# A fused attention and two-expert kernel on one core: weights decoded in place, one scale for the first output weights, and the pooled sums of twelve head pairs by accumulating transfers

## The chip, the cores and the metric

The kernel runs on one core of one Trainium2 chip. TensorE (PE) multiplies matrices, VectorE (DVE) and ScalarE (ACT) do the elementwise work, SyncE (SP) issues the loads and stores, and GpSimd (POOL) does next to nothing before the change. The metric is the device time of one launch in microseconds.

## What is computed

```python
def sm_attn(qq, kk, vv): ...          # softmax(qq kk^T / sqrt(64)) vv
q_d, k_d, v_d = (a.reshape(4, 8, 144, 4, 64).mean(axis=3) for a in (q, k, v))
out_up = np.repeat(sm_attn(q_d, k_d, v_d), 4, axis=2)       # coarse attention, 144 positions
mask = np.abs(pos[:, None] - pos[None, :]) < 4              # local attention, 576 positions
out_local = softmax(where(mask, scale * q @ k.T, -1e9)) @ v
x = (out_up + out_local).transpose(0, 2, 1, 3).reshape(2304, 512)
x = softplus(x @ w1_in) @ w1_out                            # 512 -> 2048 -> 512, weights in float64
h = x @ w2_in
out = (h * cos(h)) @ w2_out
```

q, k and v are FP32, batch 4, 8 heads, 576 positions. The result must hold far more than 16-bit precision, so each large product is made of three FP16 products of high and low halves (high by high, high by low, low by high).

## The kernel before

**Attention** works on 16 pairs of heads, `pair(b, c)`: batch b, heads 2c and 2c + 1. SP loads three layouts of a pair: `qk` (q and k by head dimension), `vd` (v as 72 partitions by the four positions of a pool) and `vw` (v in windows of 64). VectorE pools by four (`sum1` and `sum2` write `qd`, `sum3` and `sum4` write `vs`). TensorE makes local scores (`A`, tiles `any`) and coarse scores (`Bm`, from `qd`), ScalarE and VectorE the softmaxes, TensorE transposes (`Cm`, `Dm`) and multiplies by v (`Em`); `E1` adds both parts into a tile `xt` of the experts' input.

**Tokens** come in five tiles, four of 512 and one of 256 (`TILES`). Tile 0 needs the four pairs of batch 0, tile 1 those of batches 0 and 1. The sixteen pairs stand at steps written out by hand (`POS1` to `POS3`) among the units of the experts.

**Weights** come as raw 64-bit floats, in eight blocks of 128 x 1024 for each of w1i, w1o, w2i and w2o. `decode` makes FP32 of a block: ScalarE `rebase`, VectorE `join1` and `join2`, ScalarE `bound` (the sum of absolute values, for a safe scale). `scale` gets the maximum over partitions by a spread on TensorE (`allmax`, a broadcast column times `ident_s`) and a reduction on VectorE, and `split` writes the FP16 halves: `high` on ScalarE or VectorE, `low` on VectorE. Before the change the FP32 block is a buffer `x` of its own, and each block of w1i has its own scale. w1o is scaled in four groups of four f, so tile 0's layer 2 is gathered in four accumulations, joined on VectorE (`y_out`).

**Layers.** `unit_in` is one slice f of 128 hidden columns of layer 1 (or of layer 1 of the second expert): twelve matmuls `h<-xt,w1i_t`, then ScalarE and VectorE up to the halves `gh` and `gl`. `l2` and `l4` are the output layers (`any<-g,w1o_t`, `any<-w2o_t,g`). A tile's input needs its maximum, a scale and a split ahead (`x_in`, `y_in`).

**Order.** Nothing is issued where the code stands. Each operation goes into a plan with its engine, a cost and what it reads and writes; `due` gives it a due time by going back from the end, and `order` writes all engines' queues out in one sequence, ready operations by due time. Each engine runs its queue strictly in that order. Where TensorE would be idle early in the program the plan puts in multiplications of zeros (`h<-zero`), which keep its clock up.

Of the kernel before, what the change touches and what calls it, by code (L numbers as in the profile page):

```python
# [13 lines left out]
F32 = mybir.dt.float32  # L14
# [26 lines left out]
POS1 = (2, 5, 8, 11)  # L41
POS2 = (33, 37, 41, 45)
POS3 = (50, 55, 60, 65)
LAT = {"pe": 0.2, "act": 0.145, "dve": 0.13, "pool": 0.06, "sp": 0.95}
NQK, NVD, NVW, NSM, NXB, NST, NGS = 3, 2, 3, 3, 3, 2, 8
# [10 lines left out]
W2STEP = 1  # L56
# [27 lines left out]
class Plan:  # L84
# [36 lines left out]
    def due(self):  # L121
        nxt = 0.0
        for op in reversed(self.ops):
            e, cost = min(op.cost.items(), key=lambda x: x[1])
            end = min([s.due - LAT[e] for s in op.succ], default=0.0)
            if "pe" in op.cost:
                end = min(end, nxt)
                nxt = end - cost
            op.due = end - cost
# [26 lines left out]
    def order(self):  # L156
# [12 lines left out]
        def cool(cost, weight):  # L169

            if now < 0.6 or now > WARM:
                return False
            a0 = now + cost - WIN
            busy[:] = [b for b in busy if b[1] > now - WIN]
            return cost * weight + sum(max(0.0, b - max(a, a0)) * w for a, b, w in busy) < THR
# [91 lines left out]

def dma(kb):
    return {"sp": kb / 353.0}


def build(tc, qk, vw, vd, mask, w1i, w1o, w2i, w2o, out):
# [3 lines left out]
    with ExitStack() as ctx:  # L276
# [12 lines left out]
        def carr(name, n=1):  # L289
            return const.tile([128, n], F32, name=name)  # L290
# [6 lines left out]
        vmx = const.tile([128, NC_], F32, name="vmx")  # L297
# [17 lines left out]
        XB, STG = ring(dp, "x", NXB, [128, 2, 512]), ring(dp, "stg", NST, [128, 2, 512], I64)  # L315
# [52 lines left out]
        def allmax(am, n, red, reads, writes, name):  # L368
# [20 lines left out]
            P.add(pe(0.3 * n), spread, reads, [h], [h], name + " spread")  # L389
# [24 lines left out]
        class Weight:  # L414
            def __init__(self, name, dram):
                self.name, self.dram = name, dram
                self.w = [None] * NF
                self.bd, self.s = carr(f"bd_{name}", NB), carr(f"s_{name}", NF)

            def place(self, pool_):  # L420
                self.t = pool_.tile([128, NF, 2, 512], F16, name=f"{self.name}_t")

            def hi(self, f, a, n):
                return self.t[:, f, 0, a : a + n]

            def lo(self, f, a, n):
                return self.t[:, f, 1, a : a + n]
# [7 lines left out]
            def decode(self, b, after=()):  # L435

                raw, x = STG_.new(), XB_.new()
# [9 lines left out]
                def rebase():  # L447
# [6 lines left out]
                        out=x.t, in_=half(F32, 1), func=AF.Prelu, scale=float(2.0**-112), alpha=-float(2.0**32)  # L454
                    )

                def join1():
                    ts(bits(x.t), bits(x.t), 3, ALU.logical_shift_left)

                def join2():  # L460
                    nc.vector.scalar_tensor_tensor(  # L461
                        out=bits(x.t), in0=half(I32, 0), scalar=29, in1=bits(x.t),
# [3 lines left out]
                def bound():  # L466
                    nc.scalar.activation(
                        out=self.t[:, 2 * b : 2 * b + 2, 0, :].bitcast(BF16), in_=x.t, func=AF.Abs,
                        accum_out=self.bd[:, b : b + 1],
                    )  # L470

                P.add(act(1024), rebase, [raw], [x], [x], nm + " rebase")
                P.add(dve(1024, True), join1, [], [x], name=nm + " join1")
                P.add(dve(1024), join2, [raw], [x], name=nm + " join2")
                P.add(act(1024, 1), bound, [x], [("bd", self.name, b), *self.keys(b)], name=nm + " bound")
                return x
# [15 lines left out]
            def split(self, b, x):  # L492
                w, s = lambda: self.t[:, 2 * b : 2 * b + 2], self.s[:, 2 * b : 2 * b + 1]
                k = ("s", self.name, b)
                nm = f"{self.name}{b}"
                P.add(
                    {**act(1024, 1), **dve(1024, True, 1)}, lambda e: scaled(e, w()[:, :, 0, :], x.t, s),
                    [x, k], self.keys(b), name=nm + " high",
# [762 lines left out]
```

## Time and profile before

| | |
|---|---|
| three runs | 947.76 us median (947.12 to 948.87) |
| profiled execution | 947.95 us |
| its span, first to last instruction | 946.2 us |
| mean granted clock of TensorE | 0.986 |
| busy: TensorE / VectorE / ScalarE / GpSimd | 899.2 / 690.4 / 470.0 / 1.6 us |
| 133 + 72 multiplications of zeros | 34.4 + 18.7 us of TensorE |
| moved by DMA | 58.89 MB, 62 GB/s over the span |

TensorE's busy time is 95% of the span, but an average over stages with different limits; the zero multiplications count in it, too. What a change is worth is read by stages.

### The profile page before, as it was taken

Reading aid. Unit: us, or ns where it says so; the run is one execution under the profiler, and the core shown is the slowest. Engines: PE = TensorE matmul, PEld = TensorE weight load, DVE = VectorE, ACT = ScalarE, POOL = GpSimd, SP = SyncE. Lnnn points to the kernel's source line nnn. Section 1 sums busy time; section 2 is a strip of 40 time slices with the busy share of each in tenths; the row PEclk is TensorE's granted clock in tenths of the full one; section 3 lists DMA queues with packets and bytes.
Section 4 is the critical chain, followed back from the end, with each engine's and each line's share of the span. In section 5 each row is a group of like instructions: output and inputs, shape, how many; then the busy total and the mean of one; then the engine's idle time right before and its main releaser. Section 6 shows DMA issues by size and latency. Waiting matters only on the chain.

```text
span 946.2 us, 14558 instructions
## 1 busy us (share of the span) xinstructions
PE 899.2 (95%) x5809; PEld 469.7 (50%) x5809; DVE 690.4 (73%) x1474; ACT 470.0 (50%) x823; POOL 1.6 (0%) x11
## 2 busy tenths in 40 slices
PE   7899887799999999999999999999999999999797
PEld 4555443345555554444446864444444444444364
DVE  7999999976668776999964566567557656755465
ACT  3464696525445467879866632234224323422243
POOL 0000000000000000000000000000000000000000
PEclk9999998899999999999999999999999999999899
DMA  9557332400122003442200000010001000100100
GB/s 312 164 168 243 119 128 89 171 26 27 31 64 104 1 1 118 152 175 89 90 1 1 1 2 0 1 42 4 1 1 45 1 1 1 45 1 1 44 1 23
DMA packets 13363, 58.89 MB, mean 62 GB/s; under 512 B 1520, under 2 KB 1648, under 8 KB 9200
## 3 DMA queue, kind: packets, MB, share of 16 engines
q1 hardware_dynamic: 13296, 57.97, 17.7%
q8 instruction: 45, 0.74, 0.3%
q14 instruction: 22, 0.18, 0.1%
HBM read 53.25 MB, written 4.72 MB: 61 GB/s over the span
## 4 chain that ended last, share of the span: by engine, by line
PE 74%; DVE 16%; ACT 6%; DMA 2%; issue 1%; SPq 0%; ACTq 0%; DVEq 0%
PE h L897 34%; PE any L1031 19%; PE any L989 17%; DVE td L350 1%; DVE x L461 1%; PE any L724 1%; DVE sm L342 1%; DVE w1i_t L350 1%; DMA vd<-vd 1%; ACT ta L905 1%; DVE xt L350 1%; DMA qk<-qk 1%; DVE rs L602 1%; PE any L675 1%; DVE g L342 1%
## 5 line engine op out<-in xcount | busy, mean ns | idle before, releaser
L897 PE MATMUL h<-xt,w2i_t 128*128 128x512 f16 (+1 forms) x960 | 201.5, 362 | 9.5 <-DVE xt L866 5.3
L897 PE MATMUL h<-xt,w1i_t 128*128 128x512 f16 (+1 forms) x960 | 199.4, 360 | 9.3 <-DVE red L385 6.6
L1031 PE MATMUL any<-w2o_t,g 128*128 128x512 f16 x864 | 197.1, 379 | 0.3 <-DVE g L362 0.3
L989 PE MATMUL any<-g,w1o_t 128*128 128x512 f16 (+1 forms) x864 | 179.5, 357 | 2.3 <-ACT ed L646 1.4
L897 PEld LDWEIGHTS <-w2i_t 128*128 128x128 f16 x960 | 95.3, 99 | 105.7 <-issue 11.5
L897 PEld LDWEIGHTS <-w1i_t 128*128 128x128 f16 x960 | 93.8, 98 | 102.6 <-issue 14.2
L989 PEld LDWEIGHTS <-w1o_t 128*128 128x128 f16 x960 | 93.7, 98 | 89.1 <-issue 4.8
L930 ACT ACTIVATE ta<-h,quarter,i 128x512 f32<-128x512 f32 (+1 forms) x80 | 58.8, 735 | 155.2 <-PE h L897 155.2
L1031 PEld LDWEIGHTS <-g 128*128 128x128 f16 x864 | 84.5, 98 | 100.6 <-DVE g L362 0.8
L342 DVE TENSOR_TENSOR g<-td,g 128x512 f16<-128x512 f32 (+1 forms) x152 | 96.3, 634 | 8.0 <-ACT g L360 1.3
L905 ACT ACTIVATE ta<-h,i 128x512 f32<-128x512 f32 (+1 forms) x80 | 51.4, 642 | 80.7 <-PE h L897 67.4
L935 DVE TENSOR_SCALAR tb<-ta 128x512 f32<-128x512 f32 (+1 forms) x80 | 32.0, 400 | 77.6 <-ACT ta L930 77.1
L945 DVE SCALAR_TENSOR_TENSOR td<-h,r,tc 128x512 f32<-128x512 f32 (+1 forms) x80 | 55.8, 697 | 42.9 <-ACT tc L941 41.2
L941 ACT ACTIVATE tc<-ta 128x512 f32<-128x512 f32 (+1 forms) x80 | 46.9, 586 | 74.5 <-DVE ta L342 74.5
L350 DVE SCALAR_TENSOR_TENSOR td<-ta,sg,tb 128x512 f32<-128x512 f32 (+1 forms) x64 | 43.7, 682 | 48.4 <-ACT ta L917 48.0
L917 ACT ACTIVATE ta<-ta,one 128x512 f32<-128x512 f32 (+1 forms) x80 | 54.2, 680 | 2.0
L362 DVE CAST g<-td 128x512 f16<-128x512 f32 (+1 forms) x124 | 49.4, 398 | 8.0 <-PE any L989 0.8
L342 DVE TENSOR_TENSOR ta<-ta,tb 128x512 f32<-128x512 f32 (+1 forms) x80 | 51.0, 638 | 2.4
L909 ACT ACTIVATE tb<-h,r 128x512 f32<-128x512 f32 (+1 forms) x80 | 51.1, 639 | 0.0
L913 ACT ACTIVATE ta<-ta 128x512 f32<-128x512 f32 (+1 forms) x80 | 46.9, 588 | 0.0
L453 ACT ACTIVATE x<-stg 128x1024 f32<-128x1024 f32 x32 | 36.8, 1149 | 14.1 <-DVE w2i_t L350 3.8
L1195 PE MATMUL h<-zero 128*128 128x512 f16 x133 | 34.4, 393 | 5.3 <-POOL zero L1186 2.4
(147 smaller groups left out, 848.8 us busy)
## 6 DMA issues: line engine op xcount, KB each, us to landing
qk<-qk SPq DMA_DIRECT2D x16, 589.0 KB, 6.6
stg<-w1i SPq DMA_DIRECT2D x8, 1024.0 KB, 7.0
stg<-w1o SPq DMA_DIRECT2D x8, 1024.0 KB, 6.4
stg<-w2i SPq DMA_DIRECT2D x8, 1024.0 KB, 4.8
stg<-w2o SPq DMA_DIRECT2D x8, 1024.0 KB, 4.8
vw<-vw SPq DMA_DIRECT2D x16, 320.0 KB, 4.3
vd<-vd SPq DMA_DIRECT2D x16, 288.0 KB
out<-osb SPq DMA_DIRECT2D x18, 256.0 KB, 2.1
```

Source lines behind the costliest of these rows:

```text
L342: eng[e].tensor_tensor(out=out, in0=in0, in1=in1, op=op)
L350: nc.vector.scalar_tensor_tensor(out=out, in0=raw, scalar=s, in1=other, op0=ALU.mult, op1=op)
L362: nc.vector.tensor_copy(out, in_)
L897: nc.tensor.matmul(h.t[:, 0:n], l, r, start=(i == 0), stop=(i == 11))
L905: act(n, 1, True), lambda: nc.scalar.activation(out=a(), in_=h.t[:, 0:n], func=AF.Abs, scale=col(o.i1, f)),
L909: act(n, 1, True), lambda: nc.scalar.activation(out=b(), in_=h.t[:, 0:n], func=AF.Relu, scale=col(o.r1, f)),
L913: act(n), lambda: nc.scalar.activation(out=a(), in_=a(), func=AF.Exp, scale=-1.0),
L917: act(n, 1), lambda: nc.scalar.activation(out=a(), in_=a(), func=AF.Ln, bias=one),
L930: act(n, 2, True), lambda: nc.scalar.activation(out=a(), in_=h.t[:, 0:n], func=AF.Identity, scale=col(o.i2, f), bias=quarter), [h, *sc], [ ...
L945: dve(n, False, 1), lambda: nc.vector.scalar_tensor_tensor(out=td.t[:, 0:n], in0=h.t[:, 0:n], scalar=col(o.r1, f), in1=r(), op0=ALU.mult, ...
L989: nc.tensor.matmul(a.t[:, i, 0:n], l, r, start=(first and j == 0), stop=(last and j == 2))
L1031: nc.tensor.matmul(a.t[:, i], l, r, start=(f == 0 and j == 0), stop=(f == NF - 1 and j == 2))
```

## The change

Five things change together. **(1)** A block is decoded in the memory of its own FP16 halves: the weight tile has room for one half-block more, the FP32 values of block b lie over the low halves of b and the high halves of b + 1, and `split` goes through them in order. `bound` writes its by-product over the raw block. The buffers `x` and their limit go; tile 0's raw input gets a buffer of its own instead of lying in w1i. **(2)** w1i is scaled in two groups of four blocks and w1o, once all eight blocks are decoded, by one scale (`first_scale`), so layer 2 of tile 0 is one accumulation over 16 f. w2i and w2o are scaled two blocks at a time. **(3)** For batches 1 to 3 (`DA`), `qd` and `vs` come straight from memory: for each of the four positions of a pool GpSimd issues three transfers, the first time as copies, then three times adding in FP32 onto what is there. `vd` isn't loaded for them and the four sums on VectorE go. `qs` and `vr` are the same q, k and v laid out for it beforehand. **(4)** The maxima are BF16 instead of FP32, and some work that either engine could do is fixed on ScalarE (`either`). **(5)** `due` counts the load of VectorE and ScalarE, too; the pairs' positions move; the second expert prepares tile t + 1 at unit 8 of tile t, and keeps four output groups back before tile 4.

```diff
-POS1 = (2, 5, 8, 11)
+POS1 = (6, 10, 15, 20)
+W2G = 2
+QKP, VP, DA = (), (), (1, 2, 3)
+YIN = 8
+DR4 = 4
+A_W, A_C, A_X, A_G = True, True, True, False
+CAP = ("pe", "dve", "act")
+OUT0 = 8
+IN0 = ((0, 4), (4, 4))
...
+def either(a, d, first):
+    return a if first else {**a, **d}
...
-        ident_s = const.tile([128, 128], F32, name="ident_s")
+        ident_s = const.tile([128, 128], BF16, name="ident_s")
...
+                self.t = pool_.tile([128, 1024 * (NF + 1)], F16, name=f"{self.name}_t")
...
+            def floats(self, b):
+                return self.t[:, 2048 * b + 1024 : 2048 * b + 3072].bitcast(F32).rearrange("p (m e) -> p m e", m=2)
...
                 P.add(
-                    {**act(1024, 1), **dve(1024, True, 1)}, lambda e: scaled(e, w()[:, :, 0, :], x.t, s),
-                    [x, k], self.keys(b), name=nm + " high",
+                    either(act(1024, 1), dve(1024, True, 1), self.first and A_W), lambda e: scaled(e, self.his(b), self.floats(b), s),
+                    [x, k], self.keys(b) + over, name=nm + " high",
                 )
...
+            elif b in DA:
+                def term(r):
+                    kw = {"accum_op": ALU.add} if r else {}
+                    heads = qd.t.rearrange("p (m i) -> p m i", m=3)
+                    nc.gpsimd.dma_start(out=heads[0:64, 0:3:2, :], in_=qs[b, c, r, 0:64], **kw)
+                    nc.gpsimd.dma_start(out=heads[64:128, 1:3, :], in_=qs[b, c, r, 64:128], **kw)
+                    nc.gpsimd.dma_start(out=vs.t, in_=vr[b, c, r], **kw)
+                for r in range(4):
+                    aop(
+                        {"pool": 3.0}, lambda r=r: term(r), [], [qd, vs, "qd", "vs"], [] if r else [qd, vs], f"{nm}term{r}",
+                    )
...
-            m = 4 if t == 0 else NF
-            first, last = f % m == 0, f % m == m - 1
+            first, last = f == 0, f == NF - 1
...
+        def grp_out():
+            for b in range(NB):
+                W1O.decode(b)
+            W1O.scale(0, 4)
+            first = [("sc0", b) for b in range(NB)]
             W1O.scale(
-                2 * g, 2, group_scale(g), [("sc0", 2 * g), ("sc0", 2 * g + 1)],
-                [("sc0g", g)] + [("s", "w1o", 2 * g), ("s", "w1o", 2 * g + 1)],
+                4, 4, first_scale(), first + [("s", "w1o", b) for b in range(4)],
+                [("sc", 0)] + [("s", "w1o", b) for b in range(NB)],
             )
-            for i in range(2):
-                W1O.split(2 * g + i, xs[i])
+            for b in range(NB):
+                W1O.split(b)
...
-            if f == 0:
-                if t == 4:
-                    drain(0)
+            if i == 0:
                 y_in(t)
+            if f == YIN and t < 4:
+                y_in(t + 1)
+            if t == 4 and f == 0:
+                drain(DR4)
```

GpSimd's queue held no transfer; now it holds 144. The first two terms of the first pair of batch 1, with what each waits for (`DMASW` are the counters of its own earlier transfers; DVE and PE waits are for the last readers of the buffers):

```order
L648 DMA qd_117<-qs 64x2x144 [waits DVE_49,PE_49]
L649 DMA qd_117<-qs 64x288
L650 DMA vs_120<-vr 72x256 [waits PE_49]
L648 DMA qd_117<-qs 64x2x144 [waits DMASW0_49]
L649 DMA qd_117<-qs 64x288 [waits DMASW1_49]
L650 DMA vs_120<-vr 72x256 [waits DMASW2_49]
```

Each transfer that adds waits until the one of the term before into the same bytes has landed; two more terms like the second follow, and then the next pair into `qd_118`.

VectorE before, at the first output weights, from the reduction of the first group's maxima to its first low half:

```order
L339 TENSOR_SCALAR s_w1o<-red 128x4
L362 CAST xt_84<-td_96 128x512
L339 TENSOR_SCALAR s_w1o<-s_w1o 128x4
L342 TENSOR_TENSOR xt_84<-td_96,xt_84 128x512
L810 TENSOR_TENSOR gs<-lc_159,s_w1o 128x4
L350 SCALAR_TENSOR_TENSOR td_96<-ta_93,lc_159,tb_95 128x512
L811 TENSOR_REDUCE kg<-gs 128x1
L350 SCALAR_TENSOR_TENSOR xt_83<-xt_83,sx_179,xs_97 128x512
L339 TENSOR_SCALAR ikg<-kg 128x1
...
L356 TENSOR_SCALAR w1o_t<-x_106,s_w1o 128x2x512
L356 TENSOR_SCALAR xs_97<-xt_83,sx_179 128x512
L350 SCALAR_TENSOR_TENSOR w1o_t<-x_106,s_w1o,w1o_t 128x2x512
```

And after the change, from the second half of the common scale to the first low half:

```order
L380 TENSOR_SCALAR s_w1o<-red 128x8
L844 TENSOR_TENSOR xt_84<-any_89,up_129 128x128
L380 TENSOR_SCALAR s_w1o<-s_w1o 128x8
L383 TENSOR_TENSOR xt_85<-td_96,xt_85 128x512
L911 TENSOR_TENSOR gs<-lc_160,s_w1o 128x16
L391 SCALAR_TENSOR_TENSOR td_96<-ta_92,lc_160,tb_94 128x512
L912 TENSOR_REDUCE k_166<-gs 128x1
L403 CAST xt_86<-td_96 128x512
L380 TENSOR_SCALAR ik_167<-k_166 128x1
...
L383 TENSOR_TENSOR xt_86<-td_96,xt_86 128x512
L391 SCALAR_TENSOR_TENSOR w1o_t<-w1o_t,s_w1o 128x1024
```

The low half reads and writes `w1o_t` alone, all sixteen f share one scale, the high half ahead of it has gone to ScalarE, and the splits of tile 1 (`xt_83` with `xs_97`) have moved behind it. It was the 375th instruction of VectorE and is the 255th.

TensorE before, where tile 4 of the second expert begins (`w2o_t` with `g`: layer 4 of tile 3; `am`: the maximum of tile 4; `xt_86`: its input):

```order
L1031 LDWEIGHTS g_105
L1031 MATMUL any_88<-w2o_t,g_105 128x512
L378 MATMUL h_91<-ident_s,am_4_245 128x128
L897 LDWEIGHTS w2i_t
L897 MATMUL h_90<-xt_86,w2i_t 128x256
```

And after it:

```order
L1124 LDWEIGHTS g_101
L1124 MATMUL any_88<-w2o_t,g_101 128x512
L998 LDWEIGHTS w2i_t
L998 MATMUL h_91<-xt_86,w2i_t 128x256
...
L998 MATMUL h_90<-xt_86,w2i_t 128x256
L1124 LDWEIGHTS g_102
L1124 MATMUL any_87<-w2o_t,g_102 128x512
```

The spread of tile 4's maximum now stands several hundred rows earlier, and two units of tile 4 lie among the layer-4 groups of tile 3, four of which (`g_102` and on) come behind them.

## Rows read from the trace of the kernel before

**Rows 1.** Busy time by stretches of the span, all engines (count), granted clock, DMA share.
```profile
core 0: us, PE busy (x) PEld busy (x) DVE busy (x) ACT busy (x) POOL busy (x), PEclk, DMA share, GB/s
0.00:167.20 167.20, 143.33 (x1496) 82.74 (x1496) 157.70 (x376) 101.88 (x201) 1.64 (x11) 0.98 0.52 173
167.20:173.70 6.50, 0.79 (x2) 0.53 (x3) 6.50 (x14) 4.49 (x11) 0.00 (x0) 0.68 0.37 115
...
218.40:350.00 131.60, 130.57 (x1103) 71.72 (x1101) 97.37 (x210) 72.20 (x147) 0.00 (x0) 1.00 0.12 41
...
708.00:730.00 22.00, 21.09 (x100) 9.69 (x98) 15.00 (x38) 9.65 (x14) 0.00 (x0) 1.00 0.13 48
...
875.00:904.00 29.00, 22.25 (x104) 11.64 (x103) 12.72 (x40) 7.05 (x13) 0.00 (x0) 0.82 0.10 36
```

**Rows 2.** VectorE's groups to 167.2 us: count, busy us, mean ns, idle before.
```profile
L461 DVE SCALAR_TENSOR_TENSOR x<-stg,x 128x1024 int32<-128x1024 int32 x11 | 13.3, 1211 | 0.0
L350 DVE SCALAR_TENSOR_TENSOR td<-ta,lc,tb 128x512 f32<-128x512 f32 x16 | 11.9, 741 | 0.0
L350 DVE SCALAR_TENSOR_TENSOR w1i_t<-x,s_w1i,w1i_t 128x1024 f16<-128x1024 f32 x8 | 10.2, 1279 | 0.1
L342 DVE TENSOR_TENSOR qt<-qk 128x288 f32<-128x288 f32 x20 | 8.2, 451 | 3.9 <-DMA qk<-qk 3.9
L342 DVE TENSOR_TENSOR sm<-any,nm 128x640 f32<-128x640 f32 x10 | 8.1, 810 | 0.0
...
L339 DVE TENSOR_SCALAR x<-x 128x1024 int32<-128x1024 int32 x11 | 7.5, 685 | 0.0
...
L342 DVE TENSOR_TENSOR vd<-vd 72x512 f32<-72x512 f32 x10 | 6.7, 674 | 0.9 <-DMA vd<-vd 0.9
L342 DVE TENSOR_TENSOR qd<-qt 64x144 f32<-64x144 f32 x20 | 5.9, 297 | 0.1
...
L342 DVE TENSOR_TENSOR vs<-vd 72x256 f32<-72x256 f32 x10 | 3.9, 392 | 0.0
L362 DVE COPY aTd<-any 72x576 f32<-72x576 f32 x5 | 3.7, 747 | 0.3 <-PE any L692 0.3
...
L342 DVE TENSOR_TENSOR qd<-qt 128x144 f32<-128x144 f32 x10 | 3.1, 309 | 0.2
L350 DVE SCALAR_TENSOR_TENSOR xt<-xt,sx,xs 128x512 f16<-128x512 f32 x4 | 3.0, 745 | 0.0
...
L385 DVE TENSOR_REDUCE red<-h 128x1 f32<-128x128 f32 x10 | 2.8, 276 | 0.0
```

**Rows 3.** TensorE's groups, the first two behind 173.7 us alone, the others over the span.
```profile
L897 PE MATMUL h<-xt,w1i_t 128*128 128x256 f16 x192 | 23.1, 273 | 0.0
...
L378 PE MATMUL h<-ident_s,am 128*128 128x128 f32 x16 | 3.3, 287 | 0.2 <-DVE red L385 0.2
...
L576 PE MATMUL any<-qk 64*64 64x64 f32 x640 | 13.0, 223 | 0.0
L630 PE MATMUL any<-qd 128*96 128x144 f32 x72 | 10.9, 288 | 0.4 <-DVE sm L342 0.4
L572 PE MATMUL any<-mask_sb,ident_b 128*128 128x320 bf16 x32 | 7.1, 304 | 0.0
```

**Rows 4.** TensorE in order of time where tile 4 begins: start us, us, what.
```profile
887.89 0.39 PE L378 MATMUL h<-ident_s,am 128*128 128x128 f32 x2
891.53 0.49 PE L897 MATMUL h<-xt,w2i_t 128*128 128x256 f16 x3 [3.25 <-DVE xt L866]
...
900.29 2.72 PE L897 MATMUL h<-xt,w2i_t 128*128 128x256 f16 x12 [1.48 <-DVE td L945]
```

**Rows 5.** Transfers: count, KB each, median us from issue to landing.
```profile
qk<-qk SPq DMA_DIRECT2D x16, 589.0 KB, 6.6
stg<-w1i SPq DMA_DIRECT2D x8, 1024.0 KB, 7.0
out<-osb SPq DMA_DIRECT2D x18, 256.0 KB, 2.1
```

**Rows 6.** The issue of one transfer on SP: ns min/median/max, first and last start.
```profile
L531 SPq DMA_DIRECT2D vd<-vd x16: 321/321/437, 1.6 to 260.4; - x16
```

More of the change, by code (lines that the diff above doesn't have):

```diff
@@ L121, in due @@
     def due(self):
[L122 to L129, printed above, removed]
+        pre = {op: [] for op in self.ops}
+        for op in self.ops:
+            for x in op.succ:
+                pre[x].append(op)
+        left = {op: len(op.succ) for op in self.ops}
+        end = {op: 0.0 for op in self.ops}
+        free = dict.fromkeys(("pe", "dve", "act", "pool", "sp"), 0.0)
+        pes = [op for op in self.ops if "pe" in op.cost]
+        ready = [op for op in self.ops if not left[op] and "pe" not in op.cost]
+        n = len(self.ops)
+        while n:
+            best = None
+            cand = list(ready)
+            if pes and not left[pes[-1]]:
+                cand.append(pes[-1])
+            for op in cand:
+                for e in op.cost:
+                    x = (min(free[e], end[op]) if e in CAP else end[op], op.n)
+                    if best is None or x > best[0]:
+                        best = (x, op, e)
+            (x, _), op, e = best
+            if op is (pes[-1] if pes else None):
+                pes.pop()
+            else:
+                ready.remove(op)
+            op.due = x - op.cost[e]
+            if e in CAP:
+                free[e] = op.due
+            n -= 1
+            for q in pre[op]:
+                end[q] = min(end[q], op.due - LAT[min(q.cost, key=lambda z: q.cost[z])])
+                left[q] -= 1
+                if not left[q] and "pe" not in q.cost:
+                    ready.append(q)
         first = {}
@@ L466, in bound @@
                 def bound():
[L467 to L472, printed above, removed]
+                    out = raw.t.rearrange("p m e -> p (m e)")[:, 0:256].bitcast(BF16)
+                    with nc.allow_low_precision(reason="a bound, for the choice of a scale"):
+                        nc.scalar.activation(
+                            out=out.rearrange("p (m e) -> p m e", m=2), in_=self.floats(b), func=AF.Abs,
+                            accum_out=self.bd[:, b : b + 1],
+                        )
+                P.add(act(1024), rebase, [raw], [x], [], nm + " rebase")
                 P.add(dve(1024, True), join1, [], [x], name=nm + " join1")
                 P.add(dve(1024), join2, [raw], [x], name=nm + " join2")
-                P.add(act(1024, 1), bound, [x], [("bd", self.name, b), *self.keys(b)], name=nm + " bound")
-                return x
+                P.add(act(1024, 1), bound, [x], [("bd", self.name, b), raw], name=nm + " bound")
             def scale(self, b0, n, then=(), reads=(), writes=()):
@@ L507, in build @@
         W1O.place(wp)
-        STG_, XB_ = STG, XB
+        STG_ = STG
+        raw0 = [dp.tile([128, 512], F32, name=f"raw{c}") for c in range(NC_)]
         att_ops = []
@@ L641, in B1a @@
             def B1a():
[L642 removed]
+                nc.scalar.activation(
+                    out=nd.t[0:RB, 0:3], in_=nd.t[0:RB, 0:3], func=AF.Copy, scale=float(2.0**-7)
+                )
             def B2():
@@ L1111, in place2 @@
             dp2 = ex.enter_context(tc.tile_pool(name="dp2", bufs=1))
-            for s, n, shape, dt in ((STG2, NST2, [128, 2, 512], I64), (XB2, NXB2, [128, 2, 512], F32)):
-                s.tiles += [dp2.tile(shape, dt, name=f"{s.name}{i}") for i in range(n)]
+            STG2.tiles += [dp2.tile([128, 2, 512], I64, name=f"stg2{i}") for i in range(NST2)]
         def place3():
```

237 lines of the change are left out of this document (134 added, 103 removed).

## The prediction

> **What bounds the kernel now.** I read the busy time of the engines by stretches first [rows 1]. Three regimes show. Up to about 174 us VectorE is the bound: it is busy 157.7 of the first 167.2 us, while ScalarE is busy 101.9 and TensorE's 143.3 contain the zero matmuls that only keep it warm. Between 167.2 and 173.7 TensorE does almost nothing (0.79 us) and VectorE works without a break: the first layer-2 matmul of tile 0 waits for decoding. From 173.7 us on TensorE is the bound, 130.57 of 131.6 us in the stretch after 218.4, with short holes where a tile of the second expert begins (21.09 of 22.0) and one large one near the end (22.25 of 29.0 us at a granted clock of 0.82). So what the change takes off VectorE counts only ahead of 173.7 us, and behind it only TensorE's own work and holes count. I work out the two parts apart, split at the first layer-2 matmul of tile 0.
>
> **Part one, VectorE's queue up to the first low half of w1o.** That instruction ended at 167.2 us. The 376 VectorE instructions to there fall into 62 groups; the first and largest are in [rows 2]. Their busy columns add up to 183.9 us, because neighbours overlap, so one microsecond of a column is worth 167.2 / 183.9 = 0.909 us of time. The order of the changed kernel has 255 instructions to the same point (375 in that of before). What differs, in busy columns [rows 2]:
> - Pooled sums: 8.2 + 5.9 + 3.1 + 6.7 + 3.9 = 27.8 us for ten pairs; only the four of batch 0 keep them: 27.8 × 0.6 = -16.7.
> - Seven groups go to ScalarE (the copies of aTd, aT and up, the high halves of w1i and w1o, two of xhi0, the small scaling of nd), from 3.7 down to 0.7 us: -11.0.
> - Scaling: 14 small groups, from 2.8 (ten reductions over 128) to 0.1 us, together 11.5. Two scalings of four blocks for each matrix leave four reductions over 512 (a 640-wide one takes 0.81 us, so about 0.65 each) and some 20 steps at 0.16 to 0.19: 6.1. -5.4.
> - Placed behind this point now: three splits of tile 1 (3.0 for four, with their xhi and copies 5.2), the last two units of tile 0 (two sixteenths of 11.9, and their halves: 3.3), one pair's softmax (three at 0.81 and smaller ones: 5.0), one low half (1.3): -14.8.
> - Placed ahead of it now: five more decoded blocks, since all eight of w1o must be decoded before their common scale: 5 × (13.3 + 7.5) / 11 = +9.5.
>
> Sum: -38.4, so 145.5 × 0.909 = 132 us instead of 167.2. ScalarE takes over about 15 us there and would be busy some 117 of 132, where it was 102 of 167; an engine that full hands over late. If nothing of that delays VectorE the point is at 132, if all 11 us that moved come back as waits it is at 143; I take a third, 136, as ScalarE's queue still has 15 us of slack. In TensorE's order a spread and two small groups of a pair stand ahead of the first layer-2 matmul, and they need nothing that comes later, so 137 instead of 173.7 us: **36.7 us gained**. The 6.5 us hole behind 167.2 goes with it: it was a wait for the second group's scale, and there is no second group.
>
> **Part two, TensorE from there.** Before it lasts 946.2 - 173.7 = 772.5 us.
> - The spreads of the maxima read FP32 and now BF16, and there are 24 single matmuls where 56 records stood. 16 of them cost 3.3 us [rows 3], 56 about 11; a BF16 one over 320 columns costs 7.1 / 32 = 0.22, so 128 columns about 0.09, together 2.2: -8.9.
> - Tile 4 of the last expert: its input is prepared while tile 3 still runs, and four layer-4 groups stay behind as work. Before, the maximum's spread ended at 888.3 and the run of layer 4 began again at 903.0; in between stand only 36 matmuls 256 wide, with waits of 3.25 and 1.48 us and some at half speed [rows 4]; at the 23.1 / 192 = 0.12 us of their like [rows 3] they are 4.3 us of work. 14.7 - 4.3 = 10.4 us lost, of which I take 9.5 as saved. The three holes at tiles 1 to 3, 22.0 - 21.09 = 0.9 each [rows 1], go too: -2.7.
> - Fewer pairs have been begun by then: three score blocks ((7.1 + 13.0) / 16 = 1.26 us each), one coarse score (10.9 / 12 = 0.9) [rows 3] and one small transpose group (taken at 0.6) are still to do: +5.3. Four zero matmuls fewer: -1.0.
>
> Sum: 755.7. The six additions on VectorE that gathered tile 0's output over four groups were hidden behind TensorE, so removing them is worth nothing, and so are the pooled sums of the last seven pairs. Decoding in place frees a staging buffer one ScalarE instruction later than before; a load takes about 7 us [rows 5], 16 blocks in 132 us leave 8 for each and there are two buffers, so it costs nothing, and would cost a few us if loads grew slower beside the new transfers.
>
> **The new transfers.** Nothing in this trace shows an accumulating transfer or one issued by GpSimd. Each pair of batches 1 to 3 has four terms; a term's three transfers wait for those of the term before, so four landings follow one another, and the coarse score on TensorE, with all that is queued behind it, waits for the last. Two buffers of qd let GpSimd run two pairs ahead at most. The nearest rows are landings of 2.1 us (256 KB, nothing beside it) and 6.6 us (589 KB beside other loads) [rows 5]; these transfers have 74 KB. So a pair takes 4 × 2.1 = 8.4 us at least, and 26.4 us at the upper end, plus issues of 0.32 to 0.44 us each by SP's row [rows 6]. The time that it has: 151 of the 255 VectorE instructions stand between the coarse scores of the fifth and the ninth pair, so 151 / 255 × 133 / 4 = 20 us for a pair. By size I take a landing of 3 us, so 13 to 16 us for a pair, hidden, and 4 us in all for late hand-overs (one for each of the first four pairs).
>
> The Trainium skill ("DMA: Bandwidth & Descriptors", Anatomy of one DMA, SWDGE path) gives about 2.0 us fixed plus bytes over 436 GB/s for such a transfer; an estimate from that page is 2.2 us for 74 KB and 8.7 us for a pair, so hidden. Against the change speaks "SBUF — State Buffer" (SBUF: two separate sides): while VectorE runs in a two-port mode GpSimd cannot write descriptors, and a transfer of 620 ns took 3100 ns; 2.5 us more on every one of four landings would make an estimated 18.8 us of a pair, and the sum would stay. No run here shows either.
>
> **Sum.** 137 + 755.7 + 4 = 896.7 us of span. The profiled execution took 1.75 us more than its span (947.95 against 946.2) and stood 0.2 above the median, so **898 us**.
>
> **Rivals.**
> - *GpSimd's chain sets the pace* (ends slower). From P us for a pair, stage one loses 5 × (P - 20), as four pairs and the ninth queue behind one another. The later seven pairs come every 131.6 / 7 = 18.8 us [rows 1], and the 40 us of layer 2 on tile 0 give GpSimd a lead, so they lose 6 × (P - 18.8) - 40 when that is positive. At P = 28 (landings of 6.6 and an issue of 0.4): 40 + 15, so about 953. It decides from P = 27.5, a term of 6.9 us. For it: transfers of this size in many short rows, beside weights. Against: the long landings belong to transfers eight times as large.
> - *GpSimd's issues hold up VectorE.* 60 transfers are issued in stage one. If each held a VectorE instruction for as long as SP takes for an issue, 0.32 to 0.44 us [rows 6], VectorE would lose 19 to 26 us: 917 to 924. For it: VectorE is full there, so nothing hides it. Against: GpSimd stood still here but for the first microseconds, so no row shows that the two meet. The page on SBUF has it that the one that starts second blocks wholly, for two-port operations alone.
> - *A wait in the new order that I have not named*, worth half the gain: about 923.
>
> **How the numbers follow.** Forecast 0.70, between 886 (VectorE waits half as much as before, 128.5 + 1, all 10.4 us of tile 4 saved, no late hand-over: 129.5 + 754.8 + 1.6) and 912 (143 + 1, the three holes stay, 8 for hand-overs: 144 + 758.4 + 8 + 1.6). Issues that hold up VectorE 0.16, an unnamed wait 0.04, GpSimd's chain 0.10. From 884 to 932 holds the first three and leaves out the chain and part of the tails. A measurement of this kernel tells about 0.2% from no change (947.12 to 948.87 in three runs): faster 0.88, within it 0.02, slower 0.10.
>
> **What would show it.** Right: the first layer-2 matmul of tile 0 at 133 to 144 us, VectorE over 90% busy ahead of it; TensorE 99% busy from there to the last tile and no hole over 1 us where tile 4 begins; the coarse scores of batch 1 not waiting for a DMA. Wrong: waits of TensorE for the transfers into qd in each pair; VectorE's instructions of known shape longer than their rows of before; ScalarE the releaser of VectorE's idle time for more than 10 us in stage one.

## The result: 907.8 us, and the profile after

The changed kernel took 907.82 us (median of four runs, 902.35 to 912.29) beside 947.81 of the kernel before: a ratio of 0.9575, interval 0.9521 to 0.9628. 898 was predicted, with a range of 884 to 932. The execution that was profiled is the slowest of the four, 912.29 us with a span of 910.3. The runs of this kernel differ by 1.1%, those of before by 0.2%.

Busy time of the changed kernel's engines by stretches (columns as in [rows 1]):

```profile
0.00:157.10 157.10, 127.98 (x1282) 73.66 (x1283) 129.67 (x256) 112.87 (x224) 62.30 (x84) 0.93 0.75 219
157.10:350.00 192.90, 192.90 (x1552) 102.03 (x1550) 125.39 (x255) 103.31 (x203) 58.20 (x72) 1.00 0.29 61
...
395.00:430.00 35.00, 33.34 (x158) 15.18 (x157) 32.52 (x81) 32.99 (x51) 0.00 (x0) 1.00 0.49 178
430.00:845.00 415.00, 415.00 (x2123) 206.89 (x2121) 270.98 (x540) 169.21 (x278) 0.00 (x0) 1.00 0.02 9
845.00:875.00 30.00, 30.00 (x191) 18.47 (x190) 19.34 (x44) 11.78 (x24) 0.00 (x0) 1.00 0.01 2
```

The first layer-2 matmul of tile 0 begins at 157.07 us by the timeline, where 137 was predicted and 173.7 stood before. Behind it TensorE has no hole until 350 us and none from 430 to 875; the holes of before at the tiles of the second expert are gone [rows 1, 4]. That part lasts 910.3 - 157.1 = 753.2 us, where 755.7 was predicted. Ahead of it VectorE, the bound of part one before the change, is now idle for 27.4 of 157.1 us.

TensorE in order of time where tile 4 of the second expert begins (start us, us, what; an idle time ahead would stand in brackets):

```profile
850.99 2.75 PE L1124 MATMUL any<-w2o_t,g 128*128 128x512 f16 x12
853.58 2.78 PE L998 MATMUL h<-xt,w2i_t 128*128 128x256 f16 x24
856.20 2.11 PE L1124 MATMUL any<-w2o_t,g 128*128 128x512 f16 x9
```

What VectorE waited for is in its groups to 157.1 us (count, busy us, mean ns, then idle time ahead of the group and its releaser):

```profile
L391 DVE SCALAR_TENSOR_TENSOR td<-ta,lc,tb 128x512 f32<-128x512 f32 x14 | 10.4, 742 | 3.4 <-ACT ta L1018 3.3
L391 DVE SCALAR_TENSOR_TENSOR w1i_t<-w1i_t,s_w1i 128x1024 f16<-128x1024 f32 x8 | 10.2, 1276 | 0.6 <-ACT w1i_t L395 0.4
...
L380 DVE TENSOR_SCALAR w1o_t<-w1o_t 128x1024 int32<-128x1024 int32 x8 | 5.8, 731 | 8.0 <-ACT w1o_t L508 8.0
L380 DVE TENSOR_SCALAR w1i_t<-w1i_t 128x1024 int32<-128x1024 int32 x8 | 5.5, 688 | 3.5 <-ACT w1i_t L508 3.5
```

The instructions themselves are as long as before (742 and 1276 ns; 741 and 1279 in [rows 2]). The two lines with 8.0 and 3.5 us are `join1`, which waits for ScalarE's `rebase` (L508) of the same block. The waits of the first 160 us (in all, times, longest) say what `rebase` waits for:

```profile
POOL qd L648 <- DMA qd<-qs: 44.7, 19, 6.6
POOL qd L648 <- PE h L731: 22.7, 1, 22.7
POOL qd L648 <- PE any L731: 12.6, 1, 12.6
...
ACT w1i_t L508 <- DMA stg<-w1i: 7.7, 5, 2.7
...
ACT w1o_t L508 <- DMA stg<-w1o: 5.9, 5, 2.5
```

It waits for the raw block's load, by ScalarE's own waits for 13.6 us (7.7 and 5.9). TensorE is nowhere named as waiting for a transfer into `qd`; GpSimd, on the contrary, waits 35.3 us for TensorE to read a buffer of `qd`, so its chain is hidden. By the timeline its first six pairs begin at 25.1 to 129.4 us, one every 20.9 us; the last issue of the second ends at 67.4 and its coarse score begins at 74.4. The transfers (the queues, q1 with the loads and q0 with GpSimd's transfers: packets, MB, share of 16 engines; then as in [rows 5]), first over the whole span:

```profile
q1 hardware_dynamic: 12288, 54.43, 17.0%
q0 software_dynamic: 12864, 10.63, 7.6%
...
stg<-w1i SPq DMA_DIRECT2D x8, 1024.0 KB, 8.3
...
qd<-qs POOLq DMA_DIRECT2D x96, 72.0 KB, 3.0
...
vs<-vr POOLq DMA_DIRECT2D x48, 72.0 KB, 3.7
```

and then from 20 to 150 us:

```profile
q1 hardware_dynamic: 4463, 22.79, 49.7%
q0 software_dynamic: 6432, 5.31, 26.1%
...
stg<-w1o SPq DMA_DIRECT2D x8, 1024.0 KB, 6.8
stg<-w1i SPq DMA_DIRECT2D x6, 1024.0 KB, 6.9
...
qd<-qs POOLq DMA_DIRECT2D x48, 72.0 KB, 4.8
...
vs<-vr POOLq DMA_DIRECT2D x24, 72.0 KB, 5.1
```

A median stands on those loads alone whose landing the profile shows, and these are few: four of the eight w1i blocks here, one in the kernel before. The 8.3 us contain two loads that were issued at 11.4 and 11.9 us and landed after 9.3 and 12.7, before GpSimd's first transfer. From 20 us on a block of w1i lands after 6.9 us and one of w1o after 6.8, where 7.0 and 6.4 stood before, each from one block. So these rows do not show that loads became slower than before the change. What they show is that the loads are now on the chain of work that ended last: its pieces up to 157.1 us are loads of w1i and w1o for 36.4%, some 57 us.

### The profile page after: what moved, and what is told of

It reads as the page before. It is cut to its first block, busy times and chain, and to the rows that moved or that the text cites. A ratio compares the mean times of both kernels' runs of the same rounds, so it can differ in the third digit from the quotient of the medians.

```text
span 910.3 us, 14298 instructions
## 1 busy us (share of the span) xinstructions
PE 874.4 (96%) x5694; PEld 454.7 (50%) x5694; DVE 633.7 (70%) x1273; ACT 478.5 (53%) x856; POOL 120.5 (13%) x155
## 3 DMA queue, kind: packets, MB, share of 16 engines
q1 hardware_dynamic: 12288, 54.43, 17.0%
q0 software_dynamic: 12864, 10.63, 7.6%
## 4 chain that ended last, share of the span: by engine, by line
PE 80%; DMA 9%; ACT 7%; DVE 3%; issue 1%; SPq 0%; ACTq 0%
PE h L998 36%; PE any L1124 20%; PE any L1089 18%; DMA stg<-w1i 4%; DMA stg<-w1o 3%; ACT stg L524 2%; PE any L830 2%; DMA stg<-w2o 1%; PE any L819 1%; DMA stg<-w2i 1%; PE any L731 1%; DMA vw<-vw 1%; PE any L677 1%; PE any L779 1%; ACT ta L1006 1%
## 5 line engine op out<-in xcount | busy, mean ns | idle before, releaser
L998 PE MATMUL h<-xt,w2i_t 128*128 128x512 f16 (+1 forms) x960 | 199.0, 358 | 0.0
L1089 PE MATMUL any<-g,w1o_t 128*128 128x512 f16 (+1 forms) x864 | 176.9, 356 | 0.0
L648 POOL DMA_DIRECT2D qd<-qs x48 | 47.2, 984 | 158.8 <-PE any L731 77.0
L403 DVE CAST g<-td 128x512 f16<-128x512 f32 (+1 forms) x128 | 51.1, 399 | 7.3 <-PE any L1089 0.4
L650 POOL DMA_DIRECT2D vs<-vr x48 | 53.0, 1104 | 14.3 <-DMA vs<-vr 11.3
L649 POOL DMA_DIRECT2D qd<-qs x48 | 50.0, 1041 | 7.7 <-DMA qd<-qs 7.6
```

What stands on the lines that cost most here:

```text
L403: nc.vector.tensor_copy(out, in_)
L649: nc.gpsimd.dma_start(out=heads[64:128, 1:3, :], in_=qs[b, c, r, 64:128], **kw)
L650: nc.gpsimd.dma_start(out=vs.t, in_=vr[b, c, r], **kw)
L998: nc.tensor.matmul(h.t[:, 0:n], l, r, start=(i == 0), stop=(i == 11))
L1089: nc.tensor.matmul(a.t[:, i, 0:n], l, r, start=(first and j == 0), stop=(last and j == 2))
```

## The experiments

The miss is in part one, and three theories stood for it. **Theory 1:** the accumulating transfers take the DMA engines that the weights need. **Theory 2:** ScalarE, which was given more work, hands over late. **Theory 3:** a raw block is freed only by ScalarE's `bound`, which now writes over it, so the two raw buffers set the pace of the loads. All kernels below were timed against the kernel before on the same chip; each ratio has its 95% interval. Only the run with thin transfers and, up to the second expert, the one with the old order keep every engine's order of instructions. Every other edit lets the plan write a new order from the first 20 to 50 us on, so a few us between two of those kernels can come from the order as well as from the edit.

**The changed kernel again, and its transfers made thin.** Queues, issues and waits of the second kernel are those of the changed one; the adding terms move 8 rows each.

```diff
-                    kw = {"accum_op": ALU.add} if r else {}
+                    kw, n, m = ({"accum_op": ALU.add}, 8, 8) if r else ({}, 64, 72)
...
+                    nc.gpsimd.dma_start(out=heads[0:n, 0:3:2, :], in_=qs[b, c, r, 0:n], **kw)
+                    nc.gpsimd.dma_start(out=heads[64 : 64 + n, 1:3, :], in_=qs[b, c, r, 64 : 64 + n], **kw)
+                    nc.gpsimd.dma_start(out=vs.t[0:m], in_=vr[b, c, r, 0:m], **kw)
```

> The changed kernel once more, beside the other three on one chip. In its first profiled execution, 912.3 us, the first layer-2 matmul of tile 0 stood at 157.1 us instead of the predicted 137. Every theory: a median of 902 to 912 us, a spread near 1% again. If the executions differ in part one alone, the stretch behind that matmul keeps its 753 us and the matmul moves with the time of the execution.

> The order, the issues and the waits are those of the changed kernel; the three adding terms of each pair move 8 rows each instead of 64, 64 and 72, so three quarters of most pooled sums of batches 1 to 3 are left out of the output. Theory 1 (the adding transfers share the DMA engines with the weights, whose loads land late): the issue-to-landing time of w1i and w1o comes back from 8.3 and 6.8 us to at most 7.0 and 6.4, the first layer-2 matmul of tile 0 comes 10 us or more earlier than in the changed kernel beside it, the time is 893 to 898 us and its spread under 0.4%. Theory 2 (ScalarE, which was given more work, hands over late) and theory 3 (a raw block is freed only by ScalarE's bound, so its buffer sets the pace of the loads): the time stays within 3 us of the changed kernel, 902 to 912, with its spread.

The changed kernel took 908.64 us (905.11 to 912.53, ratio 0.9585, 0.9558 to 0.9612), the first layer-2 matmul at 156.9 us. With thin transfers it took 899.18 (898.20 to 901.76; 0.9484, 0.9463 to 0.9504), the matmul at 144.2. Its queue and transfers over the span, its loads from 20 to 150 us, and the same two waits of VectorE:

```profile
q0 software_dynamic: 5376, 3.63, 2.2%
...
qd<-qs POOLq DMA_DIRECT2D x24, 72.0 KB, 2.5
qd<-qs POOLq DMA_DIRECT2D x72, 9.0 KB, 2.7
...
stg<-w1o SPq DMA_DIRECT2D x8, 1024.0 KB, 5.1
stg<-w1i SPq DMA_DIRECT2D x6, 1024.0 KB, 5.1
...
DVE w1i_t L380 <- ACT w1i_t L508: 2.5, 1, 2.5
DVE w1o_t L380 <- ACT w1o_t L508: 1.8, 3, 1.3
```

Nothing but the rows moved has changed (GpSimd's issues last 0.90 to 1.01 us in the median, 0.95 to 1.11 before), so what the terms move costs 9.5 us. From 20 us on the loads land 1.8 and 1.7 us earlier than in the changed kernel, their part of the chain that ended last falls from 36.4% of 157.1 us to 11.4% of 144.2, and VectorE's waits for `rebase` shrink from 11.5 to 4.3 us. Theory 1 holds, with 899 a little above the time that it forecast.

Not all of it is waiting. TensorE does the same work from its last wait to the first layer-2 matmul in both kernels, and it took 16.6 us in the changed kernel (140.5 to 157.1) and 12.4 with thin transfers (131.8 to 144.2). The changed kernel first, then the thin one:

```profile
140.51 1.86 PE L1300 MATMUL any<-zero 128*128 128x512 f16 x4 [2.10 <-ACT aTd L401]
...
143.47 2.60 PE L830 MATMUL any<-aT,vw 64*64 64x58 f32 x44
...
146.40 9.46 PE L998 MATMUL h<-xt,w1i_t 128*128 128x512 f16 x36
```

```profile
131.84 1.02 PE L1300 MATMUL any<-zero 128*128 128x512 f16 x4 [1.84 <-ACT aTd L401]
...
133.44 1.49 PE L830 MATMUL any<-aT,vw 64*64 64x58 f32 x44
...
135.09 7.93 PE L998 MATMUL h<-xt,w1i_t 128*128 128x512 f16 x36
```

The granted clock was 0.53 of full speed from 140 to 150 us in the changed kernel, close to the lower of its two levels (1.2 instead of 2.4 GHz), after TensorE had been busy for 1.63 of the 5 us ahead; in the thin one it was 1.00 from 125 to 150. So 4.2 of the 12.9 us between these two executions are a slow clock behind TensorE's idle time; the rest had come about up to its last wait.

**A scratch tile for the by-product of `bound`.**

```diff
+        dump = dp.tile([128, 1024], BF16, name="dump")
...
-                    out = raw.t.rearrange("p m e -> p (m e)")[:, 0:256].bitcast(BF16)
+                    out = dump if self.first else raw.t.rearrange("p m e -> p (m e)")[:, 0:256].bitcast(BF16)
...
-                P.add(act(1024, 1), bound, [x], [("bd", self.name, b), raw], name=nm + " bound")
+                P.add(act(1024, 1), bound, [x], [("bd", self.name, b)] + ([] if self.first else [raw]), name=nm + " bound")
```

> The by-product of bound for w1i and w1o goes into a scratch tile of its own, so that a raw block is free again after VectorE's second joining step, as before the change. Theory 3 (the raw buffer, freed late, sets the pace): SP's waits for ScalarE ahead of weight loads (34.5 us for 10 of them) shrink to a third, ScalarE's waits for a raw block (7.7 and 5.9 us) go, the first layer-2 matmul of tile 0 comes 8 us or more earlier, 893 to 899 us. Theories 1 and 2: the loads are issued earlier but land no earlier by more than 3 us at the end of part one, 900 to 910 us.

It took 912.91 us (912.04 to 916.20; 0.9634, 0.9612 to 0.9656), 4 us more than the changed kernel beside it. SP's waits ahead of the weight loads, to 157 us, no longer name `bound` (first line, of the changed kernel), but VectorE's `join2`:

```profile
SPq L495 <- ACT stg L524: 34.5, 10, 9.2
...
SPq L496 <- DVE w1i_t L517: 31.0, 8, 6.8
SPq L496 <- DVE w1o_t L517: 21.1, 6, 5.3
```

They are longer than the 34.5 us for ScalarE that they replace, and ScalarE waits for w1i 9.1 us where it was 7.7. The first layer-2 matmul is 21 us earlier, at 135.5, but the plan has put less ahead of it: TensorE is busy 107.25 us there, 36.48 of them with zeros, so 70.8 us of work are done, 91.0 (127.98 - 37.03) in the changed kernel. The part behind it lasts 774.6 us instead of 753.2. So that `bound` holds the buffer is not the cause. That there are only two raw buffers is not cleared by this run: SP still waits for one to come free 14 times ahead of the 16 loads, and no run had a third. It also says that the place of that matmul alone is no measure, unless the order ahead of it is the same.

**Work that may go to VectorE again.**

```diff
-A_W, A_C, A_X, A_G = True, True, True, False
+A_W, A_C, A_X, A_G = False, False, False, False
```

> The work that the change fixed on ScalarE (the high halves of w1i and w1o, copies of the transposes, splits of tile inputs) may go to VectorE again, as the plan finds it; VectorE gets 18 instructions more. Theory 2 (ScalarE hands over late): waits of VectorE for ScalarE's high halves (8.0 and 3.5 us) go, the first layer-2 matmul of tile 0 comes 5 us or more earlier, 895 to 902 us. Theories 1 and 3: VectorE was full without them, so the matmul comes later by some of the 18 instructions' 8 to 12 us and the time is 905 to 918 us.

910.95 us (910.05 to 911.94; 0.9604, 0.9586 to 0.9622). VectorE's waits for `rebase` are 4.5 and 3.1 us, shorter, and the matmul stands at 154.9, and still nothing is gained. So theory 2 isn't borne out as it was put. The run doesn't show that ScalarE's load costs nothing, as VectorE, busy for 132 of the first 150 us there, got the work back; the last run below, with more of it on ScalarE, was slower.

**Part (3) taken out,** all pairs pooled on VectorE as before the change; then batch 1 alone taken out.

```diff
-QKP, VP, DA = (), (), (1, 2, 3)
+QKP, VP, DA = (), (), ()
```

> All sixteen pairs are pooled on VectorE again and vd is loaded for them; everything else is as in the changed kernel. It prices part (3) of the change. If the transfers' data cost 9.5 us, as the run with 8 rows said, then taking the transfers out gives these back and adds the pooled sums of six pairs to VectorE's queue, 16.7 us of columns or 15 of time: 910 to 918 us. If the 9.5 us came from something else than shared DMA engines, the whole 15 us show: 918 to 926. If VectorE is no longer the bound of part one, neither shows: 897 to 903.

> The kernel without accumulating transfers once more, beside the two others on one chip: 901 to 906 us, a ratio to the kernel before of 0.950 to 0.955.

> Batch 1 is pooled on VectorE, batches 2 and 3 by transfers, so that the first 100 us have few transfers beside the weights. Four pairs of VectorE's sums come back (11.1 us of columns, 10 of time) against some two thirds of 9.5 us of shared DMA engines: 909 to 914 us by the theory of shared engines; 917 to 920 if VectorE alone counts; under 903 if the transfers cost more early, beside the first weights, than the sums do.

Without the transfers: 903.56 us (901.60 to 905.15; 0.9524, 0.9504 to 0.9545), and timed again 902.91 (902.37 to 904.61; 0.9518, 0.9498 to 0.9538). With batch 1 alone taken out (`DA = (2, 3)`): 903.78 (901.19 to 911.33; 0.9538, 0.9504 to 0.9573). The first and the last are below what every theory expected that assigned VectorE's sums their full time, and the repetition agrees with the first: part (3) as a whole costs about 5 us. A stretch and two transfers of the first run without it:

```profile
100.00:150.00 50.00, 45.15 (x462) 24.88 (x459) 49.40 (x91) 46.78 (x80) 0.00 (x0) 1.00 0.36 128
...
stg<-w1i SPq DMA_DIRECT2D x8, 1024.0 KB, 5.3
stg<-w1o SPq DMA_DIRECT2D x8, 1024.0 KB, 5.0
```

and the same stretch of the changed kernel:

```profile
100.00:150.00 50.00, 38.44 (x256) 20.39 (x255) 39.67 (x74) 40.48 (x75) 23.59 (x29) 0.86 0.66 178
```

From 100 to 150 us, where w1o is decoded, VectorE does 49.4 us of work instead of 39.7, although it has the sums of six more pairs to make: it no longer waits for loads, and the granted clock of TensorE is 1.00 there instead of 0.86. That VectorE is full again agrees with its being the bound of part one once nothing else delays it.

**Batch 1 pooled on TensorE** (`QKP, VP, DA = (1,), (1,), (2, 3)`, branches that the kernel already had).

> Batch 1 is pooled on TensorE (eight FP32 multiplications by the identity for q and k of a pair, and the coarse product over the four unpooled v), batches 2 and 3 by transfers. TensorE has some 30 us of multiplications of zeros and 30 us of idle time ahead of the first layer-2 matmul, ScalarE gets four placements of about 0.85 us. Theory of shared engines: 900 to 905 us, with the loads of w1i at 7.0 to 7.5 us. Rival (theory 2, ScalarE): 908 to 914. Second rival: the FP32 multiplications stand in TensorE's order ahead of work that waits for TensorE, so 905 to 912 with more of TensorE's time and fewer zeros.

911.01 us (910.70 to 912.43; 0.9610, 0.9591 to 0.9629), which lies in the range of the second rival, but also in that of the first, so the time alone doesn't tell them apart. TensorE to 144.2 us:

```profile
L629 PE MATMUL any<-qk,ident 128*128 128x144 f32 x64 | 17.2, 436 | 0.0
```

TensorE's zeros fell from 37.0 us to 25.9, but the sums of q and k alone take 17.2 us there. GpSimd issues nothing before 99.6 us in this run, and from 20 us on the loads of w1i still land after 7.5 us: a late landing has other causes, too.

**The old order of the second expert.**

```diff
-            if i == 0:
+            if f == 0:
+                if t == 4:
+                    drain(0)
                 y_in(t)
-            if f == YIN and t < 4:
-                y_in(t + 1)
-            if t == 4 and f == 0:
-                drain(DR4)
```

> The second expert prepares each tile's input at its own first unit again and has no layer-4 groups kept back before tile 4; ahead of the second expert's first tiles all queues are those of the changed kernel. By the terms of the prediction (9.5 us at tile 4, three holes of 0.9 us) it is 12.2 us slower, 918 to 923 us, with TensorE holes at tile 4 of the sort seen before the change. Rival: the spreads are so much cheaper now that the wait at tile 4 has shrunk without the new order: under 6 us, 908 to 914.

921.43 us (917.90 to 923.76; 0.9714, 0.9690 to 0.9739), 13 us over the two medians of the changed kernel. In the profiled executions the part behind the first layer-2 matmul takes 768.4 us, some 15.5 more than the changed kernel's 753.2 and 752.6. The term of 12.2 us holds to a few us. TensorE at tile 4, the wait ahead in brackets:

```profile
864.20 0.80 PE L998 MATMUL h<-xt,w2i_t 128*128 128x256 f16 x3 [3.42 <-DVE xt L967]
...
872.97 2.71 PE L998 MATMUL h<-xt,w2i_t 128*128 128x256 f16 x12 [1.48 <-DVE td L1046]
```

They are the waits of before [rows 4]. This run shows one thing more. Its queues are those of the changed kernel up to the second expert, and yet the first layer-2 matmul begins at 150.6 us, not at 157.1 or 156.9: executions differ by 6 us in part one.

**Only v by transfers, and only q and k.** In the first, v of batches 1 to 3 is pooled by transfers and q and k on VectorE; in the second it is the other way round.

```diff
+            elif b in QA:
...
+            if b in VA:
+                def vterm(r):
+                    nc.gpsimd.dma_start(out=vs.t, in_=vr[b, c, r], **({"accum_op": ALU.add} if r else {}))
```

> Of batches 1 to 3 only v is pooled by transfers; q and k are pooled on VectorE as before the change. The transfers of v take the place of the load of vd and move no byte more than it, in 72 rows a term, while those of q and k come on top of qk, which the local scores need anyway. VectorE gets back six pairs' sums of q and k, 10.3 us of columns, and keeps out 6.4. Theory of shared engines, with the bytes on top as its cost: the loads of w1i and w1o land as fast as without transfers (at most 5.6 and 5.4 us) and VectorE keeps the saving: 898 to 902 us, below the 903.6 of the kernel without transfers. Rival: every accumulating transfer costs by its packets or its issue, whatever it replaces: 903 to 907 us, with loads of 6 us and more.

> The other half: q and k of batches 1 to 3 by transfers, v loaded as vd and pooled on VectorE. Bytes on top, 7.1 MB in all. Theory of shared engines: the loads of w1i and w1o land as late as in the changed kernel (over 6.5 us) and the time is 904 to 910 us. Rival (cost by issues or packets, shared by all three transfers of a term): it lies between the kernel without transfers and the changed kernel like the run with v alone, within 2 us of that run.

Only v: 903.86 us (902.66 to 907.52; 0.9531, 0.9507 to 0.9555). Only q and k: 913.07 (910.84 to 918.79; 0.9625, 0.9597 to 0.9653). First the kernel with v alone, then the one with q and k, whose last line is a wait to 145 us:

```profile
q0 software_dynamic: 4032, 3.54, 2.4%
...
stg<-w1i SPq DMA_DIRECT2D x8, 1024.0 KB, 5.7
stg<-w1o SPq DMA_DIRECT2D x8, 1024.0 KB, 5.3
```

```profile
q0 software_dynamic: 8832, 7.08, 5.3%
...
stg<-w1i SPq DMA_DIRECT2D x8, 1024.0 KB, 7.6
stg<-w1o SPq DMA_DIRECT2D x8, 1024.0 KB, 6.6
...
PE any L735 <- DMA qd<-qs: 6.4, 2, 5.6
```

The loads beside v alone are about as fast as without transfers, as theory 1 has it. Those beside q and k look slow, but each of these two medians stands on two loads, and without the one at the start w1i's is 5.8 us. The times don't come out: v alone gains nothing over no transfers, though 6.4 us leave VectorE, and q and k alone are worse than all three. There TensorE does wait for GpSimd's chain, 6.4 us in two waits.

**No transfers, and sixteen copies more on ScalarE** (`A_G = True` and `DA = ()`).

> No accumulating transfers, as in the kernel at 903 us, and the sixteen copies of tile 0's high halves g (0.41 us each on VectorE) fixed on ScalarE. VectorE is busy 24.4 to 25.0 of each 25 us from 25 to 150 us there, ScalarE 14.4 to 24.2. If VectorE alone bounds part one, its 3.3 us of copies ahead of the first layer-2 matmul and as much behind it are saved: 897 to 900 us. If ScalarE is the next bound beside it, which the run with v alone hints at (6.4 us taken off VectorE, and no gain), the time stays at 902 to 906 us.

911.02 us (909.93 to 913.40; 0.9601, 0.9582 to 0.9620), 8 us slower than the kernel it was made from. From 100 to 150 us neither engine is full:

```profile
100.00:150.00 50.00, 43.61 (x400) 24.75 (x401) 45.56 (x90) 45.64 (x86) 0.00 (x0) 0.90 0.40 141
```

VectorE lost 3.8 us of work in this stretch against the 49.40 above and ScalarE has 1.1 less, too, and TensorE's granted clock is 0.90 instead of 1.00. Neither of its two forecasts was right, and which wait costs the 8 us isn't shown.

## Why the prediction was right, and where it was not

**Part two was right, by its terms.** It was put at 755.7 us and took 753.2 and, in the second profiled execution, 752.6. The spreads were put at -8.9 and cost 3.80 us behind the split instead of 10.69, so -6.9: a BF16 spread stands in the trace with 0.16 us (3.80 / 24), not 0.09. Tile 4 and the three holes, 12.2 us together, are 13 by the run with the old order, some 15.5 in its profiled execution. So the two errors partly cancel, and the terms for the pairs (+5.3) and the zeros (-1.0) were not measured by themselves: 2.5 us in 755 is a little better than the terms deserve.

**Part one was too short by 12 to 16 us.** 137 and 4 for hand-overs were predicted and 157.1 measured in the slowest execution; by the two medians of the changed kernel (908.2 on average, 2 of them outside the span) it is 908.2 - 2 - 753 = 153. By the prediction's own signs it failed, too: the first layer-2 matmul is later than 144 us, VectorE is busy 83% and not over 90% ahead of it, and ScalarE is named as releaser for at least 17.5 us of VectorE's idle time (8.0, 3.5, 3.3 and 2.7), over the ten that were the sign of being wrong. That the total still lies in the range is the width of the range, not this part of the mechanism.

The step that failed is the one on the loads: "16 blocks in 132 us leave 8 for each and there are two buffers, so it costs nothing, and would cost a few us if loads grew slower beside the new transfers". The size of a load was right: 6.9 and 6.8 us from 20 us on, where about 7 was taken (from [rows 5], a median that stands on one landing). But it did not cost nothing. A raw block's buffer is held for the load and then for `rebase`, both joins and `bound`, and its next load can only be issued behind these (SP waits ten times for `bound`, 34.5 us in all, ahead of the sixteen loads); with two buffers the loads stood on the chain that ended last for 57 us of part one. The run with thin transfers, whose loads land after 5.1 us, prices what the terms move at 9.5 us, the slow clock behind TensorE's idle time included. Its first layer-2 matmul, at 144.2, is 3 us behind the forecast's 137 + 4, so that is most of the miss. I had counted a term's transfers by their landing and never as a load on the 16 engines. From 20 to 150 us their queue takes 26.1% of these engines, beside 49.7% for the loads' queue, which leaves little room where loads come together: in the stretch 50 to 75 us the DMA share is 0.97.

**The pooled sums were oversized.** They stood in the sum with -16.7 us of VectorE's columns, 15 us of time. With thin transfers they are worth 899.2 against 903.2 without transfers, 4 us; with the real ones -5. VectorE's queue isn't the only bound once it is shorter: in the thin run ScalarE is busy 49.1 of the 50 us from 100 to 150. The loose end is on the other side: by my terms a kernel without transfers should take 898 + 15 - 4 = 909 us, and it takes 903. Its order is its own, with 81.3 us of TensorE's work (118.23 - 36.90) ahead of the first layer-2 matmul at 143.2 where the changed kernel has 91.0, and the profiles don't say which term of (2), (4) or (5) was too small by 6 us. That stays open.

**The rivals.** GpSimd's chain does not set the pace, but it came closer than I had it: 20.9 us for a pair in part one, where I took 13 to 16, because a landing took 4.8 and 5.1 us in the median from 20 to 150 us, where I took 3, and an issue a microsecond and not 0.3 to 0.4; 12.6 us of these pairs are GpSimd's wait for a buffer. TensorE was slower still, with coarse scores of the fifth to the ninth pair from 51.3 to 155.8 us, 26.1 us apart, and that hid the chain. In the kernel with q and k alone TensorE waits 5.6 us for the first pair, from whose first issue at 25.0 us to its coarse score at 51.1 it takes 26 us. That pair has no lead, so it waits although the pace stays under the 27.5 us from which the rival decides: six pairs begin there from 25.0 to 132.5 us, 21.5 us apart. GpSimd's issues do not hold up VectorE: the low halves and the `td` operations last what they did before, to 3 ns in 1279. The unnamed wait did come, if the one for the loads is counted as it, at 9.5 us of the 25 that I gave it.

The Trainium skill ("DMA: Bandwidth & Descriptors", Anatomy of one DMA, SWDGE path) gave an estimate of 2.2 us for 74 KB; landings of 3.0 and 3.7 us in the median were measured over the span, 4.8 and 5.1 beside the weight loads, and 2.7 for 9 KB in the thin run, so the fixed part is the larger one here. The Trainium skill ("DMA: Bandwidth & Descriptors", SWDGE vs HWDGE vs iDMA) says that both kinds of queue feed each DMA engine, which takes turns between their queues; loads that land 1.8 and 1.7 us earlier when the terms move less agree with that. The Trainium skill ("SBUF — State Buffer", SBUF: two separate sides) would have GpSimd's transfers wait for VectorE's two-port operations; no row shows such a wait. The landings of part one are long where VectorE is busy 83% of the time, but in the thin run, where it is busy 89%, they are shorter: 4.0 us for 72 KB and 3.5 for 9 KB from 20 to 150 us.

**A better kernel** than both is the changed one without part (3): 903 us timed twice, with intervals of the ratio (0.9504 to 0.9545, 0.9498 to 0.9538) below the changed kernel's in its second timing (0.9558 to 0.9612); that of its first four runs, 0.9521 to 0.9628, is too wide to tell.

## What to carry to other kernels

Work that is moved from an engine into transfers is paid on the DMA engines: add up its share of them in the stretch where other loads are waited for, not only its landing time, and ask whether it replaces a load or comes on top. A load that is no longer than the time left for it still costs if its buffer is held long after it has landed: follow a buffer from one load to the next. A queue that is shortened by 15 us is worth 15 us only as far as the next queue allows; read the second-busiest engine and the loads in the same stretch before taking the whole. Hold apart the stretches with different limits: the terms read from the stretch in which TensorE is the bound came out within 2.5 us in 755 together.

## What the hardware showed unexpectedly

A transfer from GpSimd's queue is dear for its size: 12864 packets with 10.63 MB took 7.6% of 16 engines over 910.3 us, 104 us of one engine for a MB (0.076 x 16 x 910.3 / 10.63), where the loads in q1 took 45 (0.170 x 16 x 910.3 / 54.43). That is the adding terms more than the copies: the thin run leaves 7.00 MB of adding out and its queue took 2.2% over 896.2 us, so these took 113 us for a MB, an estimate ((0.076 x 910.3 - 0.022 x 896.2) x 16 / 7.00). Whether the adding or the short rows make it so isn't shown. An issue on GpSimd lasts 0.95 to 1.11 us in the median, where SP needs 0.32 [rows 6]; those that wait for nothing overlap and begin 0.5 to 0.6 us apart (40.56, 41.08 and 41.62 us by the timeline). Nine KB land hardly sooner than 72: 2.7 and 2.5 us over the span of one run, 3.5 and 4.0 from 20 to 150 us. And a late load was paid twice: TensorE's idle time behind it was followed by a lower granted clock, which cost 4.2 us more in work behind the last wait. The executions of the changed kernel differ by 1%, but those of the run with the work free for VectorE, which has the same transfers, by 0.2%, so the transfers alone do not account for it.
